# Softmax attention and linear attention on one core: where the last output block accumulates its first terms, and the constants of the order

## The chip, the cores and the metric

The kernel runs on one core of one Trainium2 chip. The metric is the device time of one execution in microseconds (us). A kernel is run several times, in rounds that alternate with the kernel before on the same chip; the median is quoted. A profile is one execution, and its span (first to last instruction) is about 2 us shorter than the time of the same execution. All runs used here are of the fast state. In most kernels an occasional run is 2 to 4.5 us longer, some of these at a mean TensorE clock of 0.991 to 0.994 instead of 0.996 to 1.000; they move no median.

## The reference

Two independent problems on 2048 rows of 512 columns, results side by side. Part A is attention with 32 query heads of size 16 and one key/value head; part B is linear attention with softmax features.

```python
def _A_ref(x, wq, wk, wv, wo):            # H = 32, Dh = 16
    q = (x @ wq)  # -> b h q d
    k = x @ wk;  v = x @ wv               # one head
    p = _softmax(einsum("bhqd,bkd->bhqk", q, k) * Dh ** -0.5)
    o = einsum("bhqk,bkd->bhqd", p, v)
    return o.reshape(B, S, H * Dh) @ wo
def _B_ref(x, wqkv, w_phi, wo):           # H = 32
    ...                                   # phi = softmax features of q and k
    num = einsum("bhqf,bhfd->bhqd", phi_q, kv)
    den = einsum("bhqf,bhf->bhq", phi_q, z)[..., None] + 1e-6
    return (num / den).reshape(B, S, D) @ wo
return concatenate([a, b], axis=-1)
```

The work that counts is part A's exponentials: 32 x 2048 x 2048 scores, 2048 tiles of 128x512.

## The kernel before

It computes score tiles on TensorE into banks of PSUM (the memory that TensorE writes its sums to) and exponentiates them on two routes. ScalarE takes two tiles in one instruction (`expo`, results in PT). VectorE turns a tile into bits of an approximate exponential (`bits`); GpSimd makes three shifted copies of a quad of four such tiles (`shift`); products of both routes (PT products, and products of shifted bits) add up in an accumulation bank.

```python
def expo(self, n0, us, b0):
    self.add("act", lambda a: a.activation(out=PT[:, sl[0]:sl[0] + size, :], in_=ps[:, b0:b0 + size, :], func=ACT.Exp), ...)
...
    def bits():
        self.add("dve", lambda v: v.tensor_scalar(out=o, in0=ps[:, bank, :], scalar1=self.Z1, scalar2=self.Z0, op0=ALU.mult, op1=ALU.add), ...)
...
    for t in (1, 2, 3):
        left = max(self.te["pool"] - self.fin, 0.0) + self.PSHIFT * self.pooled
        eng = "pool" if left < self.PLEFT else "dve"
```

Which tile goes which way is decided when the program is built. A planner keeps, for each engine, a list of jobs with assumed lengths and ranks, plays them through, and emits the instructions in the order that comes out. The constants below steer it: AHEAD and DBUSY decide when VectorE may take another tile, and a TensorE job with a rank above 2 that has been ready for longer than AGE gets the rank AGED and overtakes.

```python
    if sc < 32 and ... and 16 - self.at[sc] - self.dt[sc] >= self.AHEAD and ...:
        return sc                                     # a scan with room for one more quad
...
    if self.dbusy > self.DBUSY or self.dz_out >= self.NOUT:
        return False
...
def rank(self, o):
    ...
        if p > 2 and s - max(j.rel, j.since) > self.AGE:
            p = self.AGED
```

Attention is done in 32 groups of heads and rows. Each is normalized at its end: denominators go out by DMA, VectorE inverts them (job `rc`), they come back spread over partitions by DMA (denS), VectorE multiplies (job `on`). The second of a pair goes through Ot and one more DMA into On. The last group, 31, has no time for that and is normalized in place with a shuffle and two ScalarE functions (Ln, then Exp of the negative).

```python
def finish_sc2(self, sc):
    self.add("dve", lambda v: v.reciprocal(out=denC[:, r, :], in_=denC[:, r, :]), ...)
    ...                                                # DMAs denS<-denC, then denS<-denS
def finish_sc3(self, sc):
    self.add("dve", lambda v: v.tensor_tensor(out=o, in0=accS[:, r, :], in1=R[:, r, :], op=ALU.mult),
             reads=[("accS", r), ("denS", r), ("row", r)], writes=[key])
```

The last output block needs 20 products in four banks: five terms for each of four row tiles. Terms 0 and 1 come from groups 24 to 27, early; 2 from groups 28 and 29, the last to reach On by DMA; 4 from group 30, 5 from group 31.

```python
def out_part(self, i):       # banks 1 and 3: two terms early, result copied to a side buffer `part`
    ...
def out_first(self, i):      # banks 0 and 2: three terms, left in the bank
    self.add("pe", self.product(i, [(self.On[:, a, :], a) for a in range(3)], True, False), ...)
def finish_last(self):
    for i in (1, 3, 0, 2):   # 2 + 2 + 1 + 1 products, before the shuffle of group 31
        ...
    for h in range(2):       # shuffle, Ln, Exp, multiply, then the last term of two banks
        ...
    for i in range(4):       # banks to outA: ScalarE copies 0 and 2, VectorE adds `part` to 1 and 3
        ...
    for i in range(4):       # four output transfers, the third issued by ScalarE, the others by SyncE
        ...
```

Of the kernel before, what the change touches and what calls it, by code (L numbers as in the profile page):

```python
# [6 lines left out]
ALU = mybir.AluOpType  # L7
# [1153 lines left out]
class _Fast:  # L1161
# [15 lines left out]
    def __init__(self, nc, st, ins, out):  # L1177
# [59 lines left out]
        self.part = self.BxT[:, 0:2, :].rearrange("p a n -> p (a n)").bitcast(F32).rearrange("p (i n) -> p i n", i=4)  # L1237
# [292 lines left out]
    def jobs_a(self):  # L1530
# [24 lines left out]
        for i in range(2):  # L1555
            job(("pp", i), "pe", 0.43, (lambda i: (lambda: self.out_part(i)))(i), mode="full", nb=1, prio=3.0,
                after=[("on", 24 + a) for a in range(4)] + [("bk", 15), ("bv", 15)] + [("bq", 3, G) for G in range(4)])
            job(("ppc", i), "dve", 0.60, (lambda i: (lambda: self.out_part2(i)))(i), after=[("pp", i)], frees=[("pp", i)], prio=1)
            job(("fa", i), "pe", 0.65, (lambda i: (lambda: self.out_first(2 * i)))(i), mode="full", prio=3.0, after=[("on", 24 + a) for a in range(6)],
                ok=lambda: self.last_qk is not None and ("ex", self.last_qk) in self.issued)  # L1560
        for sc in range(31):
            job(("rc", sc), "dve", 0.16, (lambda sc: (lambda: self.finish_sc2(sc)))(sc), after=[("ac", sc)], prio=1.1)
            job(("on", sc), "dve", 0.60, (lambda sc: (lambda: self.finish_sc3(sc)))(sc), prio=1.3,
                after=[("rc", sc)] + ([("op", 4 * ((sc - 12) // 8) + i) for i in range(4)] if sc >= 12 and sc % 2 == 0 else []) + ([("on", sc - 1)] if sc % 2 else []))
# [407 lines left out]
    def out_part(self, i):  # L1972
        ps, On = self.ps, self.On
        bank = self.bank(("pp", i))

        def fn(pe):
            mm = None
            for A in range(2):
                mm = pe.matmul(ps[:, bank, :], lhsT=On[:, A, i * 256 + 128:i * 256 + 256], rhs=self.wo_pad[:, A, :], start=(A == 0), stop=(A == 1))
            return mm  # L1980
        self.add("pe", fn, reads=[("On", A) for A in range(2)] + ["wo_pad", "wo_pad0"], writes=[("PS", bank)])

    def out_part2(self, i):
        bank = self.bank(("pp", i))
        self.copy(self.part[:, i, :], self.ps[:, bank, :], [("PS", bank)], [("part", i)] + [("BxT", c) for c in range(4)])

# [11 lines left out]
    def out_first(self, i):  # L1998
        self.add("pe", self.product(i, [(self.On[:, a, :], a) for a in range(3)], True, False), reads=[("On", a) for a in range(3)] + ["wo_pad", "wo_pad0"], writes=[("PS", i)])

    def finish_last(self):
        ps, lnd, part, oa, ACC, product = self.ps, self.lnd, self.part, self.outA, self.bank(("acc", 31)), self.product
        H = 256
        for i in (1, 3, 0, 2):
            terms = [(self.On[:, 2, :], 2)] if i % 2 else []
            kw = dict(writes=[("PS", i)]) if i % 2 else dict(accum=[("PS", i)])
            self.add("pe", product(i, terms + [(self.On[:, 3, :], 4)], i % 2 == 1, False), reads=[("On", a) for a in range(2, 4)] + ["wo_pad", "wo_pad0"], **kw)
# [13 lines left out]
        for i in range(4):  # L2021
# [3 lines left out]
            else:  # L2025
                self.add("dve", (lambda i, o: (lambda v: v.tensor_tensor(out=o, in0=ps[:, i, :], in1=part[:, i // 2, :], op=ALU.add)))(i, o),
                         reads=[("PS", i), ("part", i // 2)], writes=[("outA", i)])
# [27 lines left out]
    def jobs_b(self, t0, t1):  # L2055
# [12 lines left out]
        for st in range(16):  # L2068
# [3 lines left out]
            if st % 4 == 3:  # L2072
                job(("bm", st), "dve", 0.34, self.b_bm, after=[("rs", st)], prio=1.9)
# [525 lines left out]
```

## Time and profile before

| | before |
|---|---|
| median | 706.76 us (705.87 to 708.95, 3 runs) |
| span of the profiled run, clock | 704.5 us, 0.999 |
| exponentials on ScalarE (two tiles each) | 706 |
| first exponential begins, last one ends | 9.07, 695.09 us |
| tail (last exponential's end to span's end) | 9.4 us |

The prediction below shows the page's groups, the waits and the ScalarE timeline. Two more places matter later. The first is where ScalarE runs dry most. This is the ScalarE timeline of the kernel before; columns are start, length, engine, line, operation, tiles, count, and in brackets the idle time before with what ended it.

```profile
319.71 1.96 ACT L1705 ACTIVATE f_PT<-f_ps 128x1024 bf16<-128x1024 f32 x2
322.12 1.02 ACT L1705 ACTIVATE f_PT<-f_ps 128x1024 bf16<-128x1024 f32 x1 [0.45 <-PE f_ps L1648]
323.72 10.19 ACT L1705 ACTIVATE f_PT<-f_ps 128x1024 bf16<-128x1024 f32 x11 [0.57 <-PE f_ps L1648]
```

Three exponentials take 4.0 us from 319.71 instead of 2.75, so 1.3 us are lost here, just after VectorE spent 3.38 us on part B's key-value sums (the job "kvfin", 315.66). The second place is VectorE in the tail of the kernel before:

```profile
694.81 0.69 DVE L1937 TENSOR_TENSOR f_On<-f_accS,f_denS 128x512 bf16<-128x512 f32 x1 [6.76 <-DMA f_denS<-f_denS]
...
695.61 0.44 DVE L2010 STREAM_SHUFFLE f_ET<-f_ps 128x256 f32<-128x256 f32 x1
```

VectorE waits 6.76 us for the denominators of group 30. They come just in time: the multiplication ends at 695.50, and the shuffle of group 31 follows at once at 695.61, when the last PT product (ends 695.5) is done.

To compare orders I use one rule throughout. An exponential takes a step of 0.9165 us and a pair of 128x512 ones 0.956 us (start to next start, 318.76 to 319.71 and its like), 32 pairs in all.  The pairs and the 0.2 us by which the last exponential outlasts a step make 30.8 us. So **head and losses** = end of the last exponential - 0.9165 x count - 30.8. For the kernel before that is 695.09 - 647.05 - 30.8 = 17.2 us, of which 9.1 is the head. The head alone varies by 0.6 us between runs of one order, so only the sum is used.

### The profile page before, as it was taken

The page shows a single profiled execution, that of the slowest core. Times are in us where ns is not written, and L with a number is a line of the kernel's source. Part 1 is how long each engine was busy: PE and PEld are TensorE (multiplying, and loading weights), DVE is VectorE, ACT ScalarE, POOL GpSimd, SP SyncE. Part 2 cuts the span into 40 slices and gives each one's busy share as a digit, 9 for nine tenths or more (in the row PEclk, how much of TensorE's full clock was granted, in tenths as well). Part 3 has the DMA queues.
Part 4 walks back from the last instruction along what each step waited for, and adds up shares of the span by engine and source line. Part 5 has one row for each costly group of instructions (what it writes and reads, how often), then busy time and mean ns, then how long its engine had stood idle before and what let it go on. Part 6 is the DMA issues. An engine that isn't in the chain of part 4 may idle for free.

```text
span 704.5 us, 20334 instructions
## 1 busy us (share of the span) xinstructions
PE 678.6 (96%) x8614; PEld 205.4 (29%) x8614; DVE 609.7 (87%) x1017; ACT 686.6 (97%) x778; POOL 513.9 (73%) x513
## 2 busy tenths in 40 slices
PE   9999999999999999998999999999999999999996
PEld 3222232232222222232223332232333222332222
DVE  4797899999999999997788688898898988899982
ACT  5999999999999999999999999999999999999996
POOL 5388778777777878876776578677667788767982
PEclk9999999999999999999999999999999999999999
DMA  6612223110112110111001210112110121110112
GB/s 126 147 11 37 38 39 77 14 9 7 10 10 28 25 7 9 12 12 9 10 6 13 47 17 14 18 10 28 17 21 10 26 34 17 14 17 21 17 17 45
DMA packets 47899, 18.43 MB, mean 26 GB/s; under 512 B 38708, under 2 KB 45940, under 8 KB 47800
## 3 DMA queue, kind: packets, MB, share of 16 engines
q1 hardware_dynamic: 45544, 16.36, 18.0%
q8 instruction: 69, 1.13, 0.7%
q10 hardware_dynamic: 2256, 0.69, 0.4%
q14 instruction: 30, 0.25, 0.1%
HBM read 2.28 MB, written 4.19 MB: 9 GB/s over the span
## 4 chain that ended last, share of the span: by engine, by line
ACT 45%; PE 43%; DVE 8%; DMA 1%; SPq 1%; issue 1%; POOL 0%; DVEq 0%; POOLq 0%
ACT f_PT L1705 43%; PE f_ps L1648 15%; PE f_ps L1870 12%; PE f_ps L1752 6%; DVE f_Z L1810 4%; PE f_ps L1959 1%; PE f_ps L2330 1%; PE f_ps L2173 1%; PE f_ps L2130 1%; ACT f_ET L2242 1%; PE f_ps L1630 1%; PE f_ps L2236 1%; ACT f_Ek L2138 1%; PE f_ps L1443 1%; DVE f_vS L2183 1%
## 5 line engine op out<-in xcount | busy, mean ns | idle before, releaser
L1705 ACT ACTIVATE f_PT<-f_ps 128x1024 bf16<-128x1024 f32 x706 | 658.1, 1107 | 4.4 <-PE f_ps L1648 3.3
L1840 POOL INT64_ADD f_Z<-f_Z x477 | 504.5, 1058 | 174.7 <-DVE f_Z L1810 135.4
L1810 DVE TENSOR_SCALAR f_Z<-f_ps 128x512 int16<-128x512 f32 x636 | 420.4, 682 | 55.9 <-PE f_ps L1648 51.6
L1648 PE MATMUL f_ps<-f_QA,f_KR 32*128 32x512 bf16 x2048 | 284.5, 384 | 11.6 <-ACT f_PT L1705 7.6
L1870 PE MATMUL f_ps<-f_Z,f_VK 128*32 128x512 f16 x2544 | 224.0, 386 | 5.7 <-PE f_ps L1870 3.1
L1648 PEld LDWEIGHTS f_ps<-f_QA,f_KR 32*128 32x128 bf16 x2048 | 71.5, 91 | 270.9 <-ACT f_PT L1705 242.9
L1752 PE MATMUL f_ps<-f_PT,f_VA 128*32 128x512 bf16 x1412 | 132.7, 385 | 0.3 <-DVE f_Z L1810 0.2
L1870 PEld LDWEIGHTS f_ps<-f_Z,f_VK 128*32 128x32 bf16 x2544 | 54.1, 94 | 101.8 <-issue 69.1
L1752 PEld LDWEIGHTS f_ps<-f_PT,f_VA 128*32 128x32 bf16 x1412 | 33.7, 94 | 48.3 <-issue 43.5
L2297 DVE TENSOR_TENSOR f_Wk<-f_ps,f_wq 128x512 bf16<-128x512 f32 x32 | 21.7, 683 | 1.7 <-PE f_ps L2286 1.4
L1449 DVE COPY f_accS<-f_ps 128x512 f32<-128x512 f32 x31 | 21.1, 680 | 0.6 <-PE f_ps L1752 0.6
L2183 DVE TENSOR_TENSOR f_vS<-f_ps,f_rs 128x1024 bf16<-128x1024 f32 x16 | 20.9, 1306 | 0.2 <-PE f_ps L2173 0.2
L2173 PE MATMUL f_ps<-f_Bwv,f_BxT 128*32 128x512 bf16 x256 | 19.6, 383 | 0.5
L2236 PE MATMUL f_ps<-f_BxT,f_Wq 128*32 128x512 bf16 x256 | 19.6, 382 | 0.2
L2130 PE MATMUL f_ps<-f_Wk,f_BxT 128*32 128x512 bf16 x256 | 19.6, 383 | 0.0
L2330 PE MATMUL f_ps<-f_Bwo,f_oT 128*32 128x512 bf16 x256 | 19.6, 383 | 0.0
L1630 PE MATMUL f_ps<-f_AxT,f_wq 128*32 128x512 bf16 (+1 forms) x272 | 19.4, 370 | 0.1
L2144 DVE TENSOR_REDUCE f_ssum<-f_Ek 128x64 f32<-128x1024 bf16 x16 | 19.3, 1206 | 0.0
L2138 ACT ACTIVATE f_Ek<-f_ps 128x512 bf16<-128x512 f32 x32 | 18.9, 700 | 0.0
L1937 DVE TENSOR_TENSOR f_On<-f_accS,f_denS 128x512 bf16<-128x512 f32 x16 | 13.0, 813 | 6.8 <-DMA f_denS<-f_denS 6.8
L2242 ACT ACTIVATE f_ET<-f_ps 128x512 bf16<-128x512 f32 x32 | 18.8, 693 | 0.0
L1443 PE MATMUL f_ps<-f_ones,f_zero 128*32 128x256 bf16 (+4 forms) x90 | 16.1, 367 | 1.3 <-POOL f_zero L1462 1.3
(96 smaller groups left out, 278.3 us busy)
## 6 DMA issues: line engine op xcount, KB each, us to landing
f_denS<-f_denS SPq DMA_DIRECT2D x124, 30.0 KB, 3.1
out_dram<-f_outB SPq DMA_DIRECT2D x16, 128.0 KB, 2.0
f_denC<-f_accS SPq DMA_DIRECT2D x124, 2.0 KB, 1.7
f_denS<-f_denC SPq DMA_DIRECT2D x124, 2.0 KB, 1.7
out_dram<-f_outA SPq DMA_DIRECT2D x15, 128.0 KB, 2.0
f_On<-f_Ot SPq DMA_DIRECT2D x60, 16.0 KB, 1.8
f_Bwv<-in_B_wqkv_dram SPq DMA_DIRECT2D x1, 512.0 KB, 4.2
f_Bwo<-in_B_wo_dram SPq DMA_DIRECT2D x1, 512.0 KB, 3.9
```

The lines of the kernel that those rows point to most:

```text
L1630: mm = pe.matmul(ps[32 * g:32 * g + 32, bank, a:a + n], lhsT=self.wq[:, dc, A * 128 + 32 * g:A * 128 + 32 * g + 32], rhs=xT[:, dc, qc * 51 ...
L1648: return pe.matmul(self.ps[:, bank, :], lhsT=self.KR[32 * g:32 * g + 32, sc % 2, kap * 128:(kap + 1) * 128], rhs=self.QA[32 * g:32 * g + 3 ...
L1705: self.add("act", lambda a: a.activation(out=PT[:, sl[0]:sl[0] + size, :], in_=ps[:, b0:b0 + size, :], func=ACT.Exp), reads=[("PS", b0 + i ...
L1752: mm = pe.matmul(ps[32 * g:32 * g + 32, bank, :], lhsT=VA[:, kap, :], rhs=PT[:, slots[g], :], start=start, stop=stop, tile_position=(0, 32 ...
L1810: self.add("dve", lambda v: v.tensor_scalar(out=o, in0=ps[:, bank, :], scalar1=self.Z1, scalar2=self.Z0, op0=ALU.mult, op1=ALU.add), reads ...
L1840: fn = lambda g: g.int64_add(out=b, in0=a, in1=256 * t * 0x1000100010001)
L1870: mm = pe.matmul(ps[32 * g:32 * g + 32, bank, :], lhsT=self.VK[:, t, kap, :], rhs=Zf[:, sl[g], :], start=start, stop=stop, tile_position=( ...
L2130: mm = pe.matmul(ps[32 * g:32 * g + 32, bank, :], lhsT=xT[:, dc, st * 128 + 32 * g:st * 128 + 32 * g + 32], rhs=w[:, dc, :], start=(dc == ...
L2173: mm = pe.matmul(ps[32 * g:32 * g + 32, bank, :], lhsT=xT[:, dc, st * 128 + 32 * g:st * 128 + 32 * g + 32], rhs=w[:, dc, :], start=(dc == ...
L2183: self.add("dve", lambda v: v.tensor_tensor(out=vS[:, :, :, 0:16], in0=v3, in1=rs.unsqueeze(3).to_broadcast([128, 2, 32, 16]), op=ALU.mult ...
L2236: mm = pe.matmul(ps[32 * g:32 * g + 32, bank, :], lhsT=w[:, dc, G * 128 + 32 * g:G * 128 + 32 * g + 32], rhs=xT[:, dc, m * 512:(m + 1) * 5 ...
L2330: mm = pe.matmul(ps[32 * g:32 * g + 32, bank, :], lhsT=oT[:, r, C, 32 * g:32 * g + 32], rhs=self.Bwo[:, C, :], start=(C == 0), stop=(C == ...
```

## The change

Its intent: the first terms of all four banks go early into score banks that the last exponentials have left, so that no side buffer and no extra copies are needed and only 8 instead of 12 products wait for the last groups of On (28 to 30). Beside that, three assumed lengths of VectorE jobs are set to measured ones, and thirteen constants of the planner are reset.

```diff
-        for i in range(2):
-            job(("pp", i), "pe", 0.43, ... self.out_part(i) ..., nb=1, prio=3.0, ...)
-            job(("ppc", i), "dve", 0.60, ... self.out_part2(i) ..., prio=1)
-            job(("fa", i), "pe", 0.65, ... self.out_first(2 * i) ..., prio=3.0, after=[("on", 24 + a) for a in range(6)], ...)
+        for i in range(4):
+            job(("fa", i), "pe", 0.43, ... self.out_first(i) ..., mode="full", prio=3.0, after=[("on", 24 + a) for a in range(4)],
+                ok=(lambda i: (lambda: self.last_qk is not None and ("ex", self.last_qk - (self.last_qk - i // 2) % 2) in self.issued))(i))
-            job(("rc", sc), "dve", 0.16, ...)
+            job(("rc", sc), "dve", 0.40, ...)
...
-                job(("bm", st), "dve", 0.34, ...)
+                job(("bm", st), "dve", 0.63, ...)
-            job(("vr", st), "dve", 0.14, ...)
+            job(("vr", st), "dve", 0.35, ...)
...
     def out_first(self, i):
-        ... terms 0, 1, 2 ...
+        ... terms 0, 1 ...
     def finish_last(self):
-        for i in (1, 3, 0, 2):
-            ...
+        for i in range(4):
+            self.add("pe", product(i, [(self.On[:, 2, :], 2), (self.On[:, 3, :], 4)], False, False), ..., accum=[("PS", i)])
...
-                self.add("dve", ... tensor_tensor(out=o, in0=ps[:, i, :], in1=part[:, i // 2, :], op=ALU.add) ...)
+                self.copy(o, ps[:, i, :], [("PS", i)], [("outA", i)])
...
-    PLEFT = 20.0
-    LOCK = ("dS", "qw", "on", "kvfin")
+    PLEFT = 8.0
+    LOCK = ("dS", "qw", "on", "k")
-    SECOND = 1.3
+    SECOND = 0.5
-    FORCE = 512
+    FORCE = 256
-    LATE = 12
+    LATE = 16
-    LEFT = 16
-    AHEAD = 4
-    AGE = 2.0
-    AGED = 0.6
-    HIGH = 16
-    DBUSY = 5.0
+    LEFT = 10
+    AHEAD = 3
+    AGE = 3.0
+    AGED = 0.8
+    HIGH = 13
+    DBUSY = 3.6
-    PATIENT = 6.0
+    PATIENT = 7.0
-    T_B = (40.0, 595.0)
+    T_B = (43.0, 575.0)
```

More of the change, by code (lines that the diff above doesn't have):

```diff
@@ L1236, in __init__ @@
         self.o_sb = self.Wk.rearrange("p a n -> p (a n)").rearrange("p (r n) -> p r n", r=2)
-        self.part = self.BxT[:, 0:2, :].rearrange("p a n -> p (a n)").bitcast(F32).rearrange("p (i n) -> p i n", i=4)
         self.lnd = self.ET[:, 0:2, :].rearrange("p a n -> p (a n)").bitcast(F32)
@@ L1554, in jobs_a @@
             job(("oa", qt), "dve", 0.60, (lambda qt: (lambda: self.outproj2(qt)))(qt), after=[("op", qt)], frees=[("op", qt)], prio=1)
-        for i in range(2):
-            job(("pp", i), "pe", 0.43, (lambda i: (lambda: self.out_part(i)))(i), mode="full", nb=1, prio=3.0,
-                after=[("on", 24 + a) for a in range(4)] + [("bk", 15), ("bv", 15)] + [("bq", 3, G) for G in range(4)])
-            job(("ppc", i), "dve", 0.60, (lambda i: (lambda: self.out_part2(i)))(i), after=[("pp", i)], frees=[("pp", i)], prio=1)
-            job(("fa", i), "pe", 0.65, (lambda i: (lambda: self.out_first(2 * i)))(i), mode="full", prio=3.0, after=[("on", 24 + a) for a in range(6)],
-                ok=lambda: self.last_qk is not None and ("ex", self.last_qk) in self.issued)
+        for i in range(4):
+            job(("fa", i), "pe", 0.43, (lambda i: (lambda: self.out_first(i)))(i), mode="full", prio=3.0, after=[("on", 24 + a) for a in range(4)],
+                ok=(lambda i: (lambda: self.last_qk is not None and ("ex", self.last_qk - (self.last_qk - i // 2) % 2) in self.issued))(i))
         for sc in range(31):
-            job(("rc", sc), "dve", 0.16, (lambda sc: (lambda: self.finish_sc2(sc)))(sc), after=[("ac", sc)], prio=1.1)
+            job(("rc", sc), "dve", 0.40, (lambda sc: (lambda: self.finish_sc2(sc)))(sc), after=[("ac", sc)], prio=1.1)
             job(("on", sc), "dve", 0.60, (lambda sc: (lambda: self.finish_sc3(sc)))(sc), prio=1.3,
@@ L1969, in outproj2 @@
         self.dmas([lambda q: q.dma_start(dst, oa[:, ring, :])], [("outA", ring)], [], 0.4, is_output=True)
-    def out_part(self, i):
-        ps, On = self.ps, self.On
-        bank = self.bank(("pp", i))
-        def fn(pe):
-            mm = None
-            for A in range(2):
-                mm = pe.matmul(ps[:, bank, :], lhsT=On[:, A, i * 256 + 128:i * 256 + 256], rhs=self.wo_pad[:, A, :], start=(A == 0), stop=(A == 1))
-            return mm
-        self.add("pe", fn, reads=[("On", A) for A in range(2)] + ["wo_pad", "wo_pad0"], writes=[("PS", bank)])
-    def out_part2(self, i):
-        bank = self.bank(("pp", i))
-        self.copy(self.part[:, i, :], self.ps[:, bank, :], [("PS", bank)], [("part", i)] + [("BxT", c) for c in range(4)])
     def product(self, i, terms, start, stop):
@@ L1998, in out_first @@
     def out_first(self, i):
-        self.add("pe", self.product(i, [(self.On[:, a, :], a) for a in range(3)], True, False), reads=[("On", a) for a in range(3)] + ["wo_pad", "wo_pad0"], writes=[("PS", i)])
+        self.add("pe", self.product(i, [(self.On[:, a, :], a) for a in range(2)], True, False), reads=[("On", a) for a in range(2)] + ["wo_pad", "wo_pad0"], writes=[("PS", i)])
     def finish_last(self):
-        ps, lnd, part, oa, ACC, product = self.ps, self.lnd, self.part, self.outA, self.bank(("acc", 31)), self.product
+        ps, lnd, oa, ACC, product = self.ps, self.lnd, self.outA, self.bank(("acc", 31)), self.product
         H = 256
-        for i in (1, 3, 0, 2):
-            terms = [(self.On[:, 2, :], 2)] if i % 2 else []
-            kw = dict(writes=[("PS", i)]) if i % 2 else dict(accum=[("PS", i)])
-            self.add("pe", product(i, terms + [(self.On[:, 3, :], 4)], i % 2 == 1, False), reads=[("On", a) for a in range(2, 4)] + ["wo_pad", "wo_pad0"], **kw)
+        for i in range(4):
+            self.add("pe", product(i, [(self.On[:, 2, :], 2), (self.On[:, 3, :], 4)], False, False), reads=[("On", a) for a in range(2, 4)] + ["wo_pad", "wo_pad0"], accum=[("PS", i)])
         for h in range(2):
@@ L2025, in finish_last @@
             else:
-                self.add("dve", (lambda i, o: (lambda v: v.tensor_tensor(out=o, in0=ps[:, i, :], in1=part[:, i // 2, :], op=ALU.add)))(i, o),
-                         reads=[("PS", i), ("part", i // 2)], writes=[("outA", i)])
+                self.copy(o, ps[:, i, :], [("PS", i)], [("outA", i)])
         for i in range(4):
@@ L2072, in jobs_b @@
             if st % 4 == 3:
-                job(("bm", st), "dve", 0.34, self.b_bm, after=[("rs", st)], prio=1.9)
+                job(("bm", st), "dve", 0.63, self.b_bm, after=[("rs", st)], prio=1.9)
             job(("rs", st), "dve", 0.46, self.b_rs, after=[("ss", st)], prio=1.9)
-            job(("vr", st), "dve", 0.14, self.b_vr, after=[("rs", st)], prio=1)
+            job(("vr", st), "dve", 0.35, self.b_vr, after=[("rs", st)], prio=1)
             job(("bv", st), "pe", 0.86, self.b_projv, after=[("fe", st)], mode="col", nb=1, prio=3)
```

## The prediction

> **What bounds the kernel now.** I read the page's busy shares first. They do not decide: three engines are above 85%.
>
> ```profile
> PE 678.6 (96%) x8614; PEld 205.4 (29%) x8614; DVE 609.7 (87%) x1017; ACT 686.6 (97%) x778; POOL 513.9 (73%) x513
> ```
>
> I then read the groups. The 2048 score tiles (128x512 each) are shared between two routes: 1412 are exponentiated on ScalarE, two per instruction (706), and 636 are turned into bits on VectorE, after which GpSimd makes three shifted copies per quad of four tiles (159 quads, 477 shifts).
>
> ```profile
> L1705 ACT ACTIVATE f_PT<-f_ps 128x1024 bf16<-128x1024 f32 x706 | 658.1, 1107 | 4.4 <-PE f_ps L1648 3.3
> L1840 POOL INT64_ADD f_Z<-f_Z x477 | 504.5, 1058 | 174.7 <-DVE f_Z L1810 135.4
> L1810 DVE TENSOR_SCALAR f_Z<-f_ps 128x512 int16<-128x512 f32 x636 | 420.4, 682 | 55.9 <-PE f_ps L1648 51.6
> ```
>
> The ScalarE timeline is the decisive view. Columns: start, length, engine, group, count.
>
> ```profile
> 9.07 68.30 ACT L1705 ACTIVATE f_PT<-f_ps 128x1024 bf16<-128x1024 f32 x74 [0.68 <-PE f_ps L1648]
> ...
> 599.04 1.24 ACT L2242 ACTIVATE f_ET<-f_ps 128x512 bf16<-128x512 f32 x2
> 599.99 95.10 ACT L1705 ACTIVATE f_PT<-f_ps 128x1024 bf16<-128x1024 f32 x103
> ```
>
> From 9.07 to 695.09 us ScalarE hardly pauses. Its own step is not the 1107 ns of one instruction, because neighbours overlap: twelve of them take 11.11 us from 80.37, and less the 0.19 us overhang of the last that is 0.91 us each. The other ScalarE work in this stretch is 32 pairs of 128x512 exponentials at 0.96 to 0.98 us a pair. The sum is 706 x 0.917 + 0.19 + 32 x 0.98 = 679.0 us out of 686.0. So about **7 us are lost** between the first and last exponential; 9.1 us lie before and 9.4 us after. The time is head + number of exponentials x 0.917 + 31.4 + losses + tail.
>
> TensorE is not the bound. In the wait table its weight loads wait for ScalarE to give back a score bank, 0.41 us each time:
>
> ```profile
> PEld f_ps L1648 <- ACT f_PT L1705: 242.9, 590, 0.8
> POOL f_Z L1840 <- DVE f_Z L1810: 135.4, 110, 16.3
> DVE f_Z L1810 <- PE f_ps L1648: 51.6, 189, 1.5
> ```
>
> Part of that wait covers the previous matmuls streaming out, but not all of it. The chain of waits that ended last names ScalarE's line first (43%), and its last ten microseconds are the tail, which the change edits:
>
> ```profile
> 692.16 2.45 SPq L1943 DMA_DIRECT2D f_On<-f_Ot  x4
> 695.14 0.40 PE L1752 MATMUL f_ps<-f_PT,f_VA 128*32 128x512 bf16 x4
> 696.87 2.77 PE L1994 MATMUL f_ps<-f_wo_pad,f_On 128*128 128x512 bf16 x12 [1.32 <-DMA f_On<-f_Ot]
> 697.73 0.42 DVE L2017 TENSOR_TENSOR f_Ot<-f_ps,f_ET 128x256 bf16<-128x256 f32 x1 [0.33 <-ACT f_ET L2015]
> 699.47 1.03 PE L1994 MATMUL f_ps<-f_wo_pad,f_Ot 128*128 128x512 bf16 x4
> ```
>
> Twelve output products wait for a transfer of On, start at 696.87, and the last four begin only at 699.47, though their operand was ready at 698.15. So products, not the last normalization, hold the end there.
>
> **What the Trainium skill says.** "Perfetto Trace Analysis", section Identifying the Most-Contended Engine, calls matmul busy time a bad measure of the distance to the limit; this trace agrees (96% busy beside 242.9 us of waiting for ScalarE). "ScalarE: Activation LUTs", section What ACT_TABLE_LOAD costs, gives an instruction with immediates 186 ns + 0.833 ns per element and an overlap of 93 ns between neighbours: 1039 and 946 ns for 1024 elements. The trace has 1107 and about 917, so more overlap than that; I use the trace. "PSUM — Partial Sum Buffer", section The four PSUM rules, says that only the first matmul of a group clears a bank's accumulate bits, later ones add. Thus a group may begin early in a bank and be continued after a wait, which the change relies on. The trace before does this already in banks 0 and 2. "VectorE: DVE Perf Modes", section The perf-mode tier table, gives 693 ns for a 16-bit tensor_scalar of 2048 elements in its 4x mode: that is what one shift would take on VectorE instead of GpSimd's 1058. No shift runs there in this trace.
>
> **The change part by part.**
>
> *Tail.* Before: 2 x 2 products early with two copies into a side buffer (656 to 658.8 us), then 6 + 4 + 2 = 12 in the tail, then 4. After: 8 early (two terms for each of four banks), then 8, then 4. The total of 20 stays. The early 8 begin when the last exponential of each bank pair has been issued. One pair's four fit into 694.2 to 695.1, where the trace has twelve filler matmuls; the other four fit between the last PT product (ends 695.5) and the landing at 696.87. A product takes (699.47 - 696.87)/12 = 0.217 us. The last four start at 696.87 + 8 x 0.217 = 698.6 instead of 699.47, above the 698.15 that their operand needs: **-0.87 us**, all on the path. The final evacuations change from tensor_tensor (685 ns) to copy (680 ns): nothing.
>
> *Side buffer.* Two VectorE copies at 0.68 us, 0.60 us apart, go: 1.2 us of VectorE, off the path. It is worth something only if VectorE uses it for more tiles. A quad costs VectorE 4 x 0.61 = 2.4 us and takes two exponentials, 1.83 us, off ScalarE; 1.2 us is half a quad, an estimate of -0.5 us at most, counted below.
>
> *Lengths.* The order is worked out when the program is built, from assumed lengths. The new ones change no instruction. The v-row reduction shows 0.35 us from start to start at 280.15 and the four-slice sum 0.64 at 261.55, so 0.35 and 0.63 are right where 0.14 and 0.34 were too short. For the reciprocal the next start is 0.16 later but the next instruction is about 0.1 longer, so 0.40 is above what I read. Under-counted VectorE work was (16 x 0.21 + 4 x 0.29 + 31 x 0.1) = 7.6 us in all; a truer plan should avoid a part of the 7 us of losses: estimate **-0.5 us**.
>
> *Knobs.* Some fifteen are reset. The lock name "k" now matches "kvfin" by its first letter, so 3.3 us of VectorE work at 315.74 keeps clear of GpSimd, once. AHEAD 3 admits one more quad late in a scan; PLEFT 8 sends a shift to VectorE when GpSimd is over 8 us behind; DBUSY 3.6 holds VectorE's queue shorter; the second stack's work ends about 20 us earlier. Their net effect is the number of quads. VectorE is idle 95 us: 16 in the first 50, 14 in the last 50 before 700, 5.5 in one wait at 391, the rest mostly 0.2 us gaps while TensorE supplies one tile per 0.9 us step. One more quad needs 2.4 us of VectorE and shortens the run by 1.83 us, so it eats 4.3 us of idle time: at best about fifteen quads if 65 us could be used. The gaps are too small and regular for that; I choose a sixth, **+2.5 quads, -4.6 us**. This is a choice: the diff doesn't tell the count, and I assume that fifteen values were kept because they helped.
>
> Sum: -0.87 - 4.6 - 0.5 = -6.0; 706.76 - 6.0 = **about 701 us**.
>
> **The rivals.**
>
> 1. *The tail alone moves.* The knobs trade one gain for another, 706 exponentials stay, and the time is 705.5 to 706. For it: the former order was already tuned, and losses are only 7 us. Against it: so many values would hardly be changed for nothing.
>
> 2. *VectorE gives more.* If short queues and earlier second-stack work let one tile go beside nearly every exponential pair, the counts would approach one to one: 682 tiles and 683 instructions, 23 fewer, -21 us, 686 us. For it: 650 to 700 us shows 42 tiles beside 50 exponentials, and GpSimd has 190 us free. Against it: from 645 to 688 us GpSimd runs without a break (3.48 us a quad against 3.66 us for four tiles at one a step), and VectorE would be over 92% busy. A third of that, 693 to 696 us, is conceivable.
>
> 3. *Shifts on VectorE eat its time.* If PLEFT 8 sends 40 of 477 there at 0.6 to 0.7 us, VectorE loses 26 us, which is ten quads of capacity or 18 us of ScalarE. For it: at most a few quads can be in flight in 14 slots, so 8 us behind does occur. Against it: they would go there mostly when VectorE had nothing else. At worst two or three quads fewer, 709 us or so.
>
> 4. *The transfer still sets the tail.* If On lands later relative to the last exponential because the order changed, the 0.87 us is lost; if it lands earlier, up to 1.2 us more is won (the last part of On is written at 695.5).
>
> **Range and chances.** The quads rule: 0 more gives 705.4, six more 694.7. I put 695 to 706 for eight in ten. Over 2% faster means under 692.6 us, seven or more quads: 0.08. Over 2% slower means above 720.9 us, which nothing here suggests: 0.015.
>
> **What would show it.** Tail: eight instead of twelve products after the On transfer, the last four 1.75 us after it, no copies into BxT. Quads: ScalarE exponentials 698 to 704 and VectorE tiles 644 to 668, with the period still 0.917. Losses: 686.0 us rule applied again, giving 5 to 7. Shifts: some tensor_scalar Z<-Z rows on VectorE. The prediction is wrong if the exponentials stay at 706 or above, if they drop below 690, or if the head of 9.07 us or the 0.917 us step moves.

## The result and the profile after

| | before | after |
|---|---|---|
| median | 706.75 us (705.87 to 708.95, 4 runs) | 702.72 us (701.80 to 703.57, 4 runs) |
| ratio of fast runs | | 0.9938, 95% interval 0.9912 to 0.9964 |
| span of the profiled run, clock | 704.5, 0.999 | 701.8, 0.996 |
| exponentials / VectorE tiles / shifts | 706 / 636 / 477 | 704 / 640 / 480 |
| last exponential ends | 695.09 | 689.00 |
| head and losses by the rule | 17.2 | 13.0 |
| tail | 9.4 | 12.8 |

A ratio is the mean time of one kernel's fast runs over that of the other's in the same rounds, so it is not quite the ratio of the medians. The result is within 2%, 4.0 us less by the medians.

The page's groups of the kernel after (the lines are four lower, as code went):

```profile
L1701 ACT ACTIVATE f_PT<-f_ps 128x1024 bf16<-128x1024 f32 x704 | 656.5, 1148 | 1.4 <-PE f_ps L1644 0.7
L1836 POOL INT64_ADD f_Z<-f_Z x480 | 505.5, 1053 | 171.9 <-DVE f_Z L1806 133.8
L1806 DVE TENSOR_SCALAR f_Z<-f_ps 128x512 int16<-128x512 f32 x640 | 424.1, 682 | 60.0 <-PE f_ps L1644 55.6
```

One quad more went to VectorE, not two and a half, and every shift is still GpSimd's: PLEFT had no effect. The mean of an exponential rose from 1107 to 1148 ns, but that is no slower engine, as the ScalarE timeline of the kernel after shows:

```profile
594.81 94.19 ACT L1701 ACTIVATE f_PT<-f_ps 128x1024 bf16<-128x1024 f32 x102
```

Less the overhang of the last one (1.15 - 0.92 = 0.23 us), 102 take 93.96 us, 0.921 each, with 0.5 us of waiting inside: the step is unchanged. An instruction whose input is ready begins earlier under the one before it and so is recorded longer: in the kernel before, the 20 of 673 that begin after the end of their neighbour last 1.02 us on average, the others up to 1.3. The longer mean is a sign of fewer waits. In the wait table TensorE now waits more for ScalarE, as one expects when ScalarE is the better-fed bound:

```profile
PEld f_ps L1644 <- ACT f_PT L1701: 260.1, 612, 1.2
```

The gain stands at the last exponential: 6.1 us earlier, 1.8 of it from two exponentials fewer and 4.2 from head and losses. Then 3.4 us are given back in the tail. The timeline of the kernel after, TensorE and VectorE from the last products on:

```profile
690.05 0.62 PE L1866 MATMUL f_ps<-f_Z,f_VK 128*32 128x512 f16 x8
...
690.49 0.39 PE L1748 MATMUL f_ps<-f_PT,f_VA 128*32 128x512 bf16 x4
692.33 0.69 DVE L1933 TENSOR_TENSOR f_On<-f_accS,f_denS 128x512 bf16<-128x512 f32 x1 [5.78 <-DMA f_denS<-f_denS]
...
693.05 0.45 DVE L1989 STREAM_SHUFFLE f_ET<-f_ps 128x256 f32<-128x256 f32 x1
...
693.12 3.39 PE L1975 MATMUL f_ps<-f_wo_pad,f_On 128*128 128x512 bf16 x8 [2.24 <-issue]
...
696.30 1.25 PE L1975 MATMUL f_ps<-f_wo_pad,f_Ot 128*128 128x512 bf16 x4
```

Eight products instead of twelve stand there, as intended. But TensorE has been idle for 2.24 us: VectorE stands in the multiplication of group 30, whose denominators land at 692.33, 3.3 us after the last exponential (before: 0.3 us before it). The shuffle of group 31 stands behind it in VectorE's order and is late as well. And the eight products take 0.42 us each instead of 0.217. The windows of the kernel after say why; columns are the window, its length, busy time of PE, PEld, DVE, ACT, POOL with counts, granted clock, DMA share, GB/s:

```profile
692.00:694.00 2.00, 0.88 (x3) 0.42 (x4) 1.60 (x5) 0.44 (x2) 0.00 (x0) 0.83 0.01 5
694.00:696.00 2.00, 2.00 (x6) 0.73 (x5) 0.85 (x2) 1.11 (x3) 0.00 (x0) 0.50 0.02 4
```

The clock fell to half in this run. "TensorE: Matmul & The Clock Gate" of the Trainium skill, section Part 1: The HAM clock gate, describes such a half-rate state after an idle window of some 3.4 us; the half rate agrees here (0.50 and 0.42 us a product), the length of the idle time is shorter (2.24 us). The profiled run is the slowest of the four (703.57), so whether the clock belongs to the kernel or to this run had to be tested.

### The profile page after: what moved, and what is told of

The parts are those of the page before. It is cut to its first block, busy times and chain, and to the rows that moved or that the text cites. A ratio compares the mean times of both kernels' runs of the same rounds, so it can differ in the third digit from the quotient of the medians.

```text
span 701.8 us, 20330 instructions
## 1 busy us (share of the span) xinstructions
PE 675.7 (96%) x8611; PEld 202.5 (29%) x8615; DVE 613.0 (87%) x1019; ACT 683.3 (97%) x776; POOL 514.8 (73%) x516
## 4 chain that ended last, share of the span: by engine, by line
ACT 48%; PE 48%; DVE 2%; issue 1%; POOL 1%; DVEq 0%; POOLq 0%
ACT f_PT L1701 46%; PE f_ps L1644 16%; PE f_ps L1866 13%; PE f_ps L1748 6%; PE f_ps L2308 2%; ACT f_Ek L2116 2%; PE f_ps L2214 2%; PE f_ps L1626 1%; PE f_ps L1955 1%; DVE f_Z L1806 1%; PE f_ps L2264 1%; PE f_ps L2289 1%; PE f_ps L1975 1%; PE f_ps L1442 1%; POOL f_Z L1836 1%
## 5 line engine op out<-in xcount | busy, mean ns | idle before, releaser
L1701 ACT ACTIVATE f_PT<-f_ps 128x1024 bf16<-128x1024 f32 x704 | 656.5, 1148 | 1.4 <-PE f_ps L1644 0.7
L1644 PE MATMUL f_ps<-f_QA,f_KR 32*128 32x512 bf16 x2048 | 280.1, 385 | 13.4 <-ACT f_PT L1701 10.2
L1644 PEld LDWEIGHTS f_ps<-f_QA,f_KR 32*128 32x128 bf16 x2048 | 69.4, 91 | 275.7 <-ACT f_PT L1701 260.1
L1933 DVE TENSOR_TENSOR f_On<-f_accS,f_denS 128x512 bf16<-128x512 f32 x16 | 15.6, 974 | 5.8 <-DMA f_denS<-f_denS 5.8
L1581 DVE TENSOR_SCALAR f_KR<-f_ps,f_half 128x512 bf16<-128x512 f32 (+2 forms) x10 | 6.0, 639 | 12.0 <-PE f_ps L1571 10.7
```

Source lines behind the costliest of these rows:

```text
L1644: return pe.matmul(self.ps[:, bank, :], lhsT=self.KR[32 * g:32 * g + 32, sc % 2, kap * 128:(kap + 1) * 128], rhs=self.QA[32 * g:32 * g + 3 ...
```

## The experiments

**Theory.** The losses fell because of lengths and constants together; the new last block is worth its 0.9 us only where the last PT product and the denominators of group 30 are in time, and in the order after they are not. **Rivals:** the new block itself gives the gain; the lock alone removes the losses; the half clock in the tail is what the tail costs.

The results in one table, each against runs of the kernel before on the same chip (their medians: 706.03 for the first four, 706.20 for the next four, 706.11 for the last four). All results were correct.

| run | exponentials | last one ends | head and losses | tail | median (runs) | ratio, 95% interval |
|---|---|---|---|---|---|---|
| tail_only | 706 | 698.79 | 20.9 | 9.6 | 706.54 (15) | 1.0003 [0.9995, 1.0012] |
| lengths_only | 710 | 696.70 | 15.2 | 10.1 | 708.55 (19) | 1.0030 [1.0022, 1.0039] |
| lengths_knobs | 704 | 689.34 | 13.3 | 10.0 | 701.17 (6) | 0.9932 [0.9911, 0.9954] |
| tail_knobs | 702 | 688.07 | 13.9 | 12.6 | 702.55 (6) | 0.9946 [0.9931, 0.9961] |
| tail_prio | 706 | 696.17 | 18.3 | 8.4 | 705.75 (22) | 0.9992 [0.9982, 1.0001] |
| after_local30 | 704 | 689.19 | 13.2 | 9.5 | 700.52 (6) | 0.9909 [0.9889, 0.9929] |
| after_fill | 704 | 689.37 | 13.4 | 11.4 | 702.76 (9) | 0.9945 [0.9926, 0.9964] |
| before_lock | 706 | 695.56 | 17.7 | 9.1 | 706.06 (22) | 0.9989 [0.9981, 0.9997] |
| after_again | 704 | 689.24 | 13.2 | 11.8 | 702.44 (10) | 0.9951 [0.9932, 0.9970] |
| after_l30_prio | 704 | 688.91 | 12.9 | 10.3 | 701.25 (7) | 0.9937 [0.9915, 0.9959] |
| best_order | 698 | 684.32 | 13.8 | 10.7 | 696.80 (5) | 0.9862 [0.9844, 0.9881] |
| best_order_q | 698 | 684.13 | 13.6 | 10.5 | 696.71 (5) | 0.9861 [0.9843, 0.9880] |

The first four columns of numbers are of one profiled run each. How far such a run can be off shows in tail_only below.

### The new last block alone (tail_only)

The change without the lengths and the constants: `"rc" 0.16`, `"bm" 0.34`, `"vr" 0.14` and all values of the planner stay as before.

> The kernel before with only the new last block (four early products pairs, no side buffer); lengths and knobs stay old. The built order still has 706 exponentials and 636 VectorE tiles. Theory (tail saves four products, 0.87 us): 705.9 us, ratio to before 0.9987, losses between first and last exponential still about 7 to 8 us. Rival (another wait takes the place, as in the changed kernel, where the tail grew from 9.4 to 12.8 us): 706.8 us or up to 709.

It came to 706.54, level with before (706.03); the rival was nearer. The timeline of tail_only:

```profile
698.01 1.89 PE L1975 MATMUL f_ps<-f_wo_pad,f_On 128*128 128x512 bf16 x8
...
699.83 0.40 PE L1748 MATMUL f_ps<-f_PT,f_VA 128*32 128x512 bf16 x4
...
700.16 1.90 PE L1975 MATMUL f_ps<-f_wo_pad,f_On 128*128 128x512 bf16 x8
...
700.29 0.44 DVE L1989 STREAM_SHUFFLE f_ET<-f_ps 128x256 f32<-128x256 f32 x1
```

All eight early products stand **before** the last PT product. It begins 1.0 us after the last exponential's end, so the shuffle comes at 1.5 us after it (before: 0.5). The four products that I had expected in the gap beside the transfer were put in front of the work that sets the end. In the planner the jobs have rank 3.0; once ready for longer than AGE they get rank AGED, 0.6, and overtake.

The profiled run of tail_only was a bad one (710.17, the longest of its 15). It shows what a lost clock costs: after the same stall as in the kernel before, the clock went to 0.50 for some 10 us.

```profile
324.00:326.00 2.00, 2.00 (x18) 0.45 (x15) 1.38 (x2) 1.80 (x2) 1.05 (x2) 0.50 0.02 1
```

The longest wait that the timeline lists for TensorE's matmuls from 314 to 324 us is 0.63 us, and the kernel before has the same waits there and keeps its clock at 1.00. That accounts for the 20.9 in the table; the 15 runs' median does not contain it.

### The lengths alone (lengths_only)

The kernel before with the three lengths of the diff and nothing else.

> The kernel before with only the three assumed lengths changed. The built order has 710 exponentials, four more. Theory (true lengths make the plan hold on the chip, so losses fall from about 8 to under 4 us): +3.7 us for the exponentials, -4 us of losses, about 706.5 us. Rival (the knobs, above all the lock on the kvfin step, removed the losses): losses stay near 8 and the time is about 710.4 us.

The order that came out has **710** exponentials, four more, and head and losses fell from 17.2 to 15.2 us. 4 x 0.917 - 2.0 = +1.6 us at the last exponential; the tail adds 0.7, as half of its late products stand before the last PT product here. It measured +2.5 us, 708.55, between the two expectations. So with truer lengths the losses fell, but with the old constants the planner also hands VectorE fewer quads (157 instead of 159); how much of the 2.0 comes from that lighter load is not separated.

### Lengths and constants, old last block (lengths_knobs)

The change without the first part of the diff.

> Lengths and knobs of the change, last block as before. The built order has 704 exponentials. Theory (the gain lies in the order, and the longer tail of the changed kernel comes from the order, not from the new products): losses 3 to 4 us and a tail of 12 us or more, 702 to 704 us. Rival (the new last block made the tail longer): tail 9.4 us as before, 700.0 us.

It came to 701.17, **faster than the kernel after**, with the same 704 exponentials and the same head and losses. My theory, a tail of 12 us or more from the order alone, was wrong: the tail is 10.0. Against the kernel before on its own chip it is 4.9 us faster, the kernel after 4.0 and 3.7 (after_again); the intervals of the ratios overlap, so the reading rests on the tails as well. The timeline of lengths_knobs:

```profile
682.54 3.70 SPq L1913 DMA_DIRECT2D f_denS<-f_denS  x4
...
686.29 2.45 SPq L1943 DMA_DIRECT2D f_On<-f_Ot  x4
...
688.69 0.69 DVE L1937 TENSOR_TENSOR f_On<-f_accS,f_denS 128x512 bf16<-128x512 f32 x1 [0.21 <-DMA f_denS<-f_denS]
...
690.71 0.45 DVE L2010 STREAM_SHUFFLE f_ET<-f_ps 128x256 f32<-128x256 f32 x1
...
691.77 2.75 PE L1994 MATMUL f_ps<-f_wo_pad,f_On 128*128 128x512 bf16 x12
...
694.36 1.03 PE L1994 MATMUL f_ps<-f_wo_pad,f_Ot 128*128 128x512 bf16 x4
```

The multiplication of group 30 waits 0.21 us for its denominators instead of 5.78, 0.7 us before the last exponential ends. Twelve late products begin at 691.77 and the end of the last four is 695.39; in the kernel after it is 697.55. The new block changes the jobs at the end and the planner orders the last 25 us differently: in the kernel after SyncE issues the four On transfers first (677.99) and the last ones of the denominators (denS from denS) from 685.72 on; in lengths_knobs the denominators' go first, from 682.54, and On's follow at 686.29. That this order of the queue makes them late is read from the two traces; no run changes it alone. The same two in the kernel after:

```profile
677.99 2.42 SPq L1939 DMA_DIRECT2D f_On<-f_Ot  x4
...
685.72 3.43 SPq L1909 DMA_DIRECT2D f_denS<-f_denS  x4
```

The old block is not at its best here either: On's transfers have landed by 689.93, but six filler matmuls (690.21 to 691.93) stand before its twelve products.

### The new block and the constants, old lengths (tail_knobs)

> New last block and knobs, old lengths. The built order has 702 exponentials, two fewer than the changed kernel. Theory (lengths remove losses): losses go back to 7 or 8 us, and with the tail as it was the time is 702.7 - 1.8 + 4 = 704.9 us. Rival (knobs remove them): losses 3 to 4 us, about 700.9 us.

It came to 702.55, between the expectations (704.9 and 700.9). Head and losses hardly rose without the lengths (13.9 against 13.3), so in this the rival, the constants, was right. 702 exponentials, the last one ending 1.3 us earlier than in lengths_knobs, and yet 1.4 us slower: the tail is 12.6 us. Here it is not the denominators. 16 leftover products of part B stand at 689.9, a backlog of 20 products of shifted bits after them, and the last PT products end at 692.9, 4.9 us after the last exponential. So in both orders with all the constants the new block lies in an end that the planner did not keep clear, for two different reasons.

### The new block with a rank that cannot age (tail_prio)

```diff
-            job(("fa", i), "pe", 0.43, ..., prio=3.0, ...
+            job(("fa", i), "pe", 0.43, ..., prio=1.9, ...
```
on tail_only.

> As tail_only (old lengths and knobs), but the early products have a rank below the age rule (prio 1.9 in place of 3.0), so that the second four no longer stand ahead of the last PT product in TensorE's order. Theory (in tail_only those four delayed the last PT product by 0.9 us, which took back the gain): the shuffle starts about 0.5 us after the last exponential instead of 1.5, the last four products end about 3.9 us after it instead of 4.7, and the time is 0.8 us under tail_only: 705.7, or down to 704.4 if the last output transfer is then issued in 0.5 us as before and not in 1.9. Rival (the place of the early products is of no account, the output transfers set the end): 706.5, the same as tail_only.

705.75 as expected, 0.45 us under before. The timeline of tail_prio:

```profile
691.09 2.45 SPq L1939 DMA_DIRECT2D f_On<-f_Ot  x4
...
696.35 0.40 PE L1748 MATMUL f_ps<-f_PT,f_VA 128*32 128x512 bf16 x4
...
696.68 2.76 PE L1975 MATMUL f_ps<-f_wo_pad,f_On 128*128 128x512 bf16 x12
...
696.81 0.44 DVE L1989 STREAM_SHUFFLE f_ET<-f_ps 128x256 f32<-128x256 f32 x1
```

The last PT product stands first now, and the shuffle begins 0.6 us after the last exponential's end (696.17). The last four products end 4.1 us after it; before they end 5.4 after (700.50 against 695.09). The tail is 8.4 instead of 9.4 us. That the early four cost the shuffle about 0.9 us where they stand before the last PT product agrees with tail_only.

It does **not** show that the new block saves products. Behind the last PT product twelve products of On stand in a row as before, the second early four and the late eight, and the last four begin 2.60 us after the first of them, as before (696.68 to 699.28; before 696.87 to 699.47). What moved is the start of the row: 0.5 us after the last exponential instead of 1.8. In this order the transfers of On are all issued by 693.54, 2.6 us before the last exponential ends; before by 694.61, 0.5 us before it. Their landing is not recorded in these two runs; where it is, it follows the issue's end by 1.2 to 2.5 us, so by my estimate On was there by 696.1, and the old block, too, could have started its row there. The head and losses of this order are 1.1 us worse by the profiled run; the medians give 0.45 us in all, and the interval of the ratio includes 1.

### Group 30 normalized without a DMA (after_local30)

The kernel after, with group 30 treated in the tail as group 31 is.

```diff
-        for sc in range(31):
+        for sc in range(30):
             job(("rc", sc), ...)
...
+        self.add("dve", lambda v: v.stream_shuffle(l30, self.accS[:, 0, :], [16] * 32), ...)
+        self.add("act", lambda a: a.activation(out=l30, in_=l30, func=ACT.Ln), ...)
+        self.add("act", lambda a: a.activation(out=l30, in_=l30, func=ACT.Exp, scale=-1.0), ...)
+        self.add("dve", lambda v: v.tensor_tensor(out=self.On[:, 3, :], in0=self.accS[:, 0, :], in1=l30, op=ALU.mult), ...)
```

> The changed kernel, with the denominators of group 30 made on the core (a VectorE shuffle, Ln and Exp on ScalarE after the last exponential) in place of three rounds of transfers. Theory (the wait for these transfers holds VectorE, hence TensorE, from 690.9 to 693.1, and the idle array then runs at half clock): no idle stretch, eight products at 0.22 us each, end about 3.4 us earlier: 699.2 us. Rival (only part of it counts, as Ln and Exp for two groups now follow each other and the last transfer's issue lengthens to 1.9 us): 700.6 us. If the transfers were not the cause: 702.7 or more.

700.52: the larger of the two expected sizes was wrong, the smaller (700.6) right. The timeline of after_local30:

```profile
690.39 0.69 DVE L1991 TENSOR_TENSOR f_On<-f_accS,f_ET 128x512 bf16<-128x512 f32 x1 [2.99 <-ACT f_ET L1990]
...
691.18 1.89 PE L1977 MATMUL f_ps<-f_wo_pad,f_On 128*128 128x512 bf16 x8
...
692.98 1.36 PE L1977 MATMUL f_ps<-f_wo_pad,f_Ot 128*128 128x512 bf16 x4
```

The hole is gone, and the eight products begin 1.9 us sooner, at full clock. With the same exponentials and the same losses, taking the wait for the denominators away is worth 2.2 us (against after_fill below, which has that wait and ran in the same rounds: 702.76). That shows what this wait in the tail of the kernel after cost.

### Ten filler products in the hole (after_fill)

```diff
+        self.fill((512,) * 10, start=False, mode="full", bank=0)
         for i in range(4):
             self.add("pe", product(i, [(self.On[:, 2, :], 2), ...
```
The filler adds zeros to bank 0.

> The changed kernel with ten filler matmuls (zero weights, accumulated into bank 0) before the eight late products, so that TensorE does not idle while VectorE waits. Theory (half of the longer tail is the clock): granted clock 1.00 to the end, eight products in 1.75 us instead of 3.2, but the last normalization is ready only at about 695.6, so some 1.3 us less: 701.4 us. Rival (the clock is not on the path, the wait is): 702.7 us.

The clock stayed at 1.00 through the tail and the median did not move (702.76 against 702.72). A window of after_fill:

```profile
694.00:696.00 2.00, 1.85 (x9) 0.62 (x8) 1.23 (x4) 1.75 (x5) 0.00 (x0) 1.00 0.01 4
```

The rival was right: the half clock is not what the median of the kernel after contains.

### The lock alone (before_lock)

```diff
-    LOCK = ("dS", "qw", "on", "kvfin")
+    LOCK = ("dS", "qw", "on", "k")
```
on the kernel before. The planner compares the first letter of a name that is a plain string, so "kvfin" never matched.

> The kernel before with only the lock name changed from kvfin to k, so that this 3.3 us step of VectorE is kept clear of GpSimd. The built order still has 706 exponentials. Theory (the stall after this step at 316 to 324 us is a part of the losses that the change removed, and the lock removes it): losses fall by 1.5 to 2 us, 704.3 us. Rival (the step stalls TensorE by its length alone, with or without the lock; the other knobs moved it to a harmless place): 706.0 us.

The rival was right in the time. The two waits after 319.71 went, others came (0.84 us lost after 333.7 by the rule), head and losses are 17.7 and the time is the same within 0.2%. The lock is not what saved the 4.2 us.

### The kernel after again (after_again)

> The kernel after, unchanged, on the same chip as the three below and with more rounds. Theory: its median is 702.7, 1.5 us above lengths_knobs (701.2 on its own chip), because in the new order the new last block waits for the denominators of group 30. Rival: the 1.5 us were the chip and the clock of single runs, and it comes in at 701.2 or below.

702.44, again 1.3 us above lengths_knobs, on another chip. The window and the timeline of after_again:

```profile
694.00:696.00 2.00, 1.85 (x9) 0.46 (x7) 1.28 (x3) 1.68 (x4) 0.00 (x0) 1.00 0.02 4
```

```profile
692.28 0.69 DVE L1933 TENSOR_TENSOR f_On<-f_accS,f_denS 128x512 bf16<-128x512 f32 x1 [5.50 <-DMA f_denS<-f_denS]
...
693.08 1.89 PE L1975 MATMUL f_ps<-f_wo_pad,f_On 128*128 128x512 bf16 x8 [1.96 <-issue]
```

The hole is there (1.96 us) with the clock at 1.00, and the tail is 11.8 us. So the wait for the denominators belongs to the kernel, and the half clock, with some 1.0 us more of tail, to the one run that was profiled first.

### Both mends together (after_l30_prio)

after_local30 with the rank of 1.9.

> after_local30 (700.5) with the early products ranked 1.9 instead of 3.0, so that they cannot age past the last PT product. Theory: what it gave in tail_only, 0.8 us, comes again: last four products end about T+4.2 after the last exponential instead of T+5.15, median 699.7. Rival: with the 704 order the two early quartets already stand where they cost nothing, and it stays at 700.5.

701.25: the theory's 699.7 missed, the rival (700.5) was nearer. The last PT product now stands before the second four early products, but a last product of shifted bits stands behind them (690.60), and the shuffle of group 31 comes at 691.06, as in after_local30 (691.13). So the last four products end at 694.28 and 694.34, all the same. Of the 0.7 us against after_local30, 0.4 are in the profiled spans, where the stretch after the last product is longer (4.9 against 4.4 us); neither that nor the rest is explained. So the rank that helped in tail_prio won nothing here.

### Fewer exponentials (best_order)

after_l30_prio with nine constants from a search over orders, for which no chip is needed as an order's count is known when it is built:

```diff
-    SECOND = 0.5     LATE = 16     LEFT = 10     AHEAD = 3     AGED = 0.8
-    HIGH = 13        PATIENT = 7.0     NEAR = 0.15     T_B = (43.0, 575.0)
+    SECOND = 0.3     LATE = 12     LEFT = 16     AHEAD = 2     AGED = 0.9
+    HIGH = 14        PATIENT = 6.0     NEAR = 0.1     T_B = (41.0, 575.0)
```

> after_local30_prio with nine constants of the planner reset to values found by a search for fewer exponentials: 698 instead of 704, 163 quads instead of 160 (489 shifts). Theory (the count of exponentials decides, losses stay near 4 us): 6 x 0.917 = 5.5 us less than after_local30_prio, 694.2 to 695.0. Rival: the extra quads are bought with waits at the quads' ends (losses 7 us or more, as in the order before), and it comes in at 697 to 700.

696.80, between theory and rival: 4.45 us less than after_l30_prio for six exponentials, 0.74 us each. The page's groups of best_order:

```profile
L1701 ACT ACTIVATE f_PT<-f_ps 128x1024 bf16<-128x1024 f32 x698 | 651.3, 1155 | 2.6 <-PE f_ps L1644 2.0
L1806 DVE TENSOR_SCALAR f_Z<-f_ps 128x512 int16<-128x512 f32 x652 | 428.8, 682 | 53.4 <-PE f_ps L1644 50.5
```

Of 6 x 0.917 = 5.5 us, 0.9 went into more losses (12.9 to 13.8) and 0.4 into the tail (10.3 to 10.7). It is the fastest kernel here together with the next one: 1.4% under the kernel before, and 5.6 us under the kernel after in the same rounds.

### Another queue for the last transfer (best_order_q)

```diff
-            ... queue="act" if i == 2 else "sp")
+            ... queue="act" if i == 3 else "sp")
```

> best_order with the fourth output transfer instead of the third issued by ScalarE, the third by SyncE. It tells whether the long last issue on SyncE (1.5 to 1.9 us instead of 0.5 where the last four products come in two pairs) belongs to the third transfer of one queue. Theory: the issue is long because it follows on the heels of another on the same queue; with the earlier transfer there, SyncE's last issue takes 0.5 us and the end comes 0.5 to 1.0 us sooner. Rival: no change (within 0.3 us), the long issue stays wherever the last transfer is.

696.71: the rival was right, nothing moved. But the premise did not occur: in both runs the long issue on SyncE (1.7 and 1.6 us) is its second, and its last takes 0.65 and 0.46 us, so the theory was hardly tested. Between the end of the last product and the end of the span lie 4.0 us (before, lengths_knobs) to 4.9 us (tail_only, after_l30_prio), and in two profiled runs of the same kernel after 4.25 and 4.8. What sets it stays open.

## Why the prediction was right or wrong

The total was right: 701.0 predicted, 702.7 measured, inside the range, within 2%. The sum behind it was not; three of its terms were off and cancelled. With after_again as the profile of the kernel after, the span changed by 701.0 - 704.5 = -3.5 us:

| term | predicted | measured | how |
|---|---|---|---|
| quads | -4.6 | -1.8 | two exponentials fewer, x 0.917 |
| lengths and losses | -0.5 | -4.0 | head and losses 17.2 to 13.2 |
| tail | -0.87 | +2.40 | 9.40 to 11.80 |

- *What bounds it.* Right. The step stayed, and every order's time followed from count, losses and tail.
- *Tail.* The sign was wrong in the kernel after. Eight late products instead of twelve came, and the last four began 1.79 us after them in after_again (693.08 to 694.87), against the predicted 1.75. But the step that failed is "start at 696.87": it took the start of the late products from the old order and moved nothing. In the new order they start 3.8 us after the last exponential instead of 1.8. That is the fourth rival, a transfer that lands later relative to the last exponential, though another one than I named: the denominators of group 30, not On. And the placing of the second four early products after the last PT product was taken for granted; in tail_only and in the kernel after they stand before it. Where both are put right (tail_prio), the tail falls by 1.0 us. That this is near the predicted 0.87 is luck: the four products were to hide in the wait for On, but On came 2.15 us earlier relative to the last exponential, twelve products in a row still followed, and only their start moved, by 1.3 us (this is the other half of the fourth rival). No run shows the block's own saving.
- *Quads.* "I choose a sixth" of the idle capacity was too much: one quad, not two and a half. The third rival did not occur: no shift went to VectorE, so PLEFT was idle, and no run shows what a shift would take there (the 693 ns stay the page's figure). Nor did the second. That there was more to be had shows in best_order with 163 quads, and its price too: 0.74 us per exponential instead of 0.917.
- *Lengths and losses.* The term mis-sized most: -0.5 against -4.0. Some 0.4 us of it are the head (9.07 to 8.69), which varies that much by itself. By themselves the lengths took 2.0 us off head and losses (and cost four exponentials), the constants with the new block 3.3, both without the block 3.9. The lock, which I had singled out, took nothing off. Between the first and the last exponential alone, the same rule gives 8.2 us lost before and 3.7 and 4.5 in the two runs of the kernel after; with the prediction's own constants it is 7.0, 2.6 and 3.4. The check that I had written down, 5 to 7, was missed on the good side. From end to end, the longest single losses before are 0.79, 0.68 and 0.56 us (at 216, 323 and 322 us); in the kernel after none is above 0.25, in after_again one is 0.45.
- *Side buffer.* Nothing is seen of the 1.2 us of VectorE, as expected.
- *Slips of the working.* The trace before does not begin the groups of banks 0 and 2 early: its only early products (656 us) are those for the side buffer, and the other twelve start together at 696.87. From 693.86 to 695.06 stand eight filler matmuls, not twelve from 694.2. Six more quads make 705.4 - 11.0 = 694.4, not 694.7. Thirteen constants are reset, not fifteen. None of these moves the total by more than 0.3 us.

What stays open: which of the constants did it. An order is one outcome of all of them together, and each alone only gives another order; only the lock was taken alone on the chip, and in tail_prio the ageing of the early products. Whether the new block saves anything where On and the denominators come late. And the 4.0 to 4.9 us after the last product.

## What to carry to other kernels

Where the order of instructions comes out of a planner, a small local change reorders the end as well: compare, in the new trace, when each input of the last block lands relative to the last instruction of the bound, before counting what the block saves. Price three things apart (how many instructions the bound runs, how long it stands idle between the first and the last, what comes after the last) and check each against the trace, because a good total can hide errors that cancel. See that a job that may fill a gap cannot overtake the work that sets the end (this brought the last PT product forward in both orders where it was tried, and helped the time at most in one of them).

## What the Trainium skill lacked or had wrong

- "ScalarE: Activation LUTs", section What ACT_TABLE_LOAD costs, gives one overlap of about 93 ns between neighbours. Here 128x1024 exponentials from PSUM with a step of 917 ns were recorded at 1107 ns in the kernel before and 1148 ns in the kernel after, so 190 and 231 ns of overlap, more where fewer waits lie between them. I found no page that says a recorded length can grow because waits went away; read as a slower engine it misleads.
- "TensorE: Matmul & The Clock Gate", section Part 1: The HAM clock gate, ties the half rate to an idle window of about 3.4 us. Here the clock was 0.50 after a pause of 2.24 us in one run (703.57 us) and 1.00 after a pause of 1.96 us in another of the same kernel; and in one run of tail_only it fell to 0.50 for some 10 us after a stretch with no listed wait of a matmul over 0.63 us, where the kernel before with the same waits kept 1.00. The page calls the window free-running and the warm-up different from run to run, which fits; the length of idleness it names does not fit the two drops. The section also describes a clock that oscillates from frequent short pauses; that comes nearer to tail_only, but names no length. The half rate lasted 3.41 us in the one run and 10.24 us in the other.
- No page that I found explains how the stretch between the last product and the end can vary as it did: bank to SBUF, issue and landing of four output transfers took 4.0 to 4.9 us here, and 4.25 and 4.8 us in two runs of one kernel.
